# Three of five pairs of forms a step later: the order of VectorE in a fused attention and feed-forward kernel

## The chip, the core and the metric

The kernel runs on one core of a Trainium2 chip. Its metric is the device time in microseconds; the time before is the median of three runs. A profile is one further execution, recorded by the hardware profiler.

## What is computed

The first half is a recurrent attention (RWKV-6) with 4 batches, 8 heads, 768 tokens and heads of 48; the second half is a feed-forward layer on its result, all in float32.

```python
for t in range(S):                       # B=4, H=8, S=768, D=48
    cur = np.einsum('bhd,bhe->bhde', u[None] * kt, vt)
    y[:, :, t] = np.einsum('bhd,bhde->bhe', rt, state + cur)
    state = wt[:, :, :, None] * state + np.einsum('bhd,bhe->bhde', kt, vt)
...
x = y.transpose(0, 2, 1, 3).reshape(B * S, H * D)   # 3072 x 384
h = x @ w_in                                         # d_ff = 2048
g = h - np.tanh(h)
return (g @ w_out)
```

## The kernel before

**Blocks and steps.** The 3072 rows are cut into 8 blocks of 384 tokens (`blocks`, index `i`: four batches, two halves `q` each). The feed-forward of a block goes through 16 slices of 128 hidden columns (`f`, 0 to 15). One pass of the inner loop is a *step*: block `i`, slice `f`, numbered `now = 16 i + f`. While block `i` is in its feed-forward, the attention of block `i + 1` (`later`) is spread over the same 16 steps, and for `i + 2` (`after`) loads and scans begin. `plan(i)` says in which step which piece is issued: `phases` (TensorE and ScalarE work of the attention), `before` and `ahead` (the `prepare` calls, mostly long VectorE instructions), `loads`.

**The order is written by hand.** Under `tc.manual_schedule` each engine executes its instructions in the order in which the Python code issues them, so the place of a call in a step is its place in the queue of its engine. Waits between the engines follow from the data.

**One step.** TensorE does `hp = x @ w_in` for the slice (`first`, L749, three products that the profile counts as six instructions); `hp` has one PSUM buffer. ScalarE copies it to `h` (L752). `slight` then makes `g = h - tanh(h)` by a short polynomial that holds for small h: `s = h*h`, `qa = (s + c)^2`, `h = TOP*h*s`, `g = REST*qa*h`. The last two are VectorE instructions (L755). They are not issued in their own step but in the next one: `rest` keeps them. From block 2 on (`fast`), and for the first 10 slices of block 7, the square is ScalarE's (L770, with L771 and L773, a pass that checks the size of s). In blocks 0 and 1 and in the last six steps of block 7 the square is VectorE's (`square`, L778), issued in its own step; `qa` follows on ScalarE a step later.

**Second product.** In blocks 0, 1 and the end of block 7 it is plain (`Second`, L826): two steps after its slice TensorE adds `g @ w_out`. From block 2 on two neighbouring slices are taken together (`Fewer`): from the parts 0a 1a 2a of the even slice's `g` and 0b 1b 2b of the odd slice's (three token groups of 128) VectorE makes ten sums and differences, the *forms*, two in one instruction of 128 x 256 (`form_g`, L796, pairs 0, 2, 4, 6, 8):

```python
G_FORMS = (("sub", "1a", "0a"), ("sub", "1a", "2a"), ("add", 0, "1b"), ("add", 1, "1b"), ("sub", 2, "0b"),
           ("sub", 3, "2b"), ("sub", "2b", 4), ("sub", 5, "0b"), ("add", "2a", 3), ("add", 0, 6))
```

A number there is an earlier form. So pair 2 reads pair 0, pair 4 reads pair 2, pair 6 pair 4, pair 8 pair 6. Similar forms of `w_out` lie in `forms`. Fifteen products of 128 x 128 (`PRODUCTS`) replace eighteen. Twelve of them go into three PSUM banks (`acc`, four products to a bank, n // 4), in two halves (`add(q, part)`): in the kernel before first n = 0 to 5, which read forms 4 to 9, two steps after the odd slice, and then n = 6 to 11, which read forms 0 to 3 and the parts 0a and 2a, a step later. With the last pair of slices of a block `scaled` has ScalarE copy the banks out (L875). The other three (`others`) are issued together, at f = 9 and at the start of the next block. Then `SUMS` adds the products up (`sum`, L897) during steps 4 to 14 of the next block, and `store` writes them out.

**Buffers.** In the tile `G` (`g_at`) the forms 0 to 3 have two sets of slots by turns, the a parts two, the b parts four, the forms 4 to 9 one (slots 14 to 19). The accumulators have one buffer, the attention's PSUM scratch (`att`) two.

**VectorE's order in a step** is:

```python
for op in rest + behind + square + formed + extra:
    op()
```

`rest` is h and g of the slice before. `behind` holds VectorE's part of the attention work that TensorE did in the step before: the masked copies (`own`, `earlier`, L454), `update_2` (ten or eleven dependent instructions on the states, L533 and L543; issued at f = 11), `others_summed` (L890, f = 2). `formed` are the form pairs: pair 0 after an even slice, pairs 2, 4, 6 and 8 after an odd one. The `prepare` calls and `sum` come at the end of the step. The results of the attention (`result 1`, L586) are TensorE's work at f = 12; they write to the PSUM tiles that `update_2` reads.

Of the kernel before, what the change touches and what calls it, by code (L numbers as in the profile page):

```python
# [46 lines left out]
ALU = mybir.AluOpType  # L47
# [3 lines left out]
B, H, S, D = 4, 8, 768, 48  # L51
P = 128
# [44 lines left out]
G_FORMS = (("sub", "1a", "0a"), ("sub", "1a", "2a"), ("add", 0, "1b"), ("add", 1, "1b"), ("sub", 2, "0b"),  # L97
           ("sub", 3, "2b"), ("sub", "2b", 4), ("sub", 5, "0b"), ("add", "2a", 3), ("add", 0, 6))
# [5 lines left out]
AHEAD_N, MAIN = 6, 12  # L104
# [16 lines left out]
def kernel(  # L121
# [12 lines left out]
    nc = tc.nc  # L134
# [65 lines left out]
    states = []  # L200
# [80 lines left out]
    class Block:  # L281
# [241 lines left out]
                                                 rhs=self.v[toks, c, e0:e0 + D], start=True, stop=True)  # L523

        def update_2(self):
            St = states[self.q]

            def tot(c):
                by = self.whole().rearrange("d (p c) -> d p c", c=NCH)[:, :, c]
                return by.unsqueeze(2).to_broadcast([P, NPAIR, D])  # L530

            def product(out, in0, c):
                nc.vector.tensor_tensor(out=out, in0=in0, in1=tot(c), op=ALU.mult)  # L533

            if self.q > 0:
                product(St[:, :, 0, 0:D], St[:, :, 0, 0:D], 0)
            for c in range(NCH - 1 if self.q == NQ - 1 else NCH):
                dst = St[:, :, c + 1, 0:D] if c + 1 < NCH else states[self.q + 1][:, :, 0, 0:D]
                kv = self.kv[c].rearrange("d (p e) -> d p e", e=D)
                if self.q == 0 and c == 0:  # L540
                    product(dst, kv, 1)
                    continue
                nc.vector.tensor_tensor(out=dst, in0=St[:, :, c, 0:D], in1=kv, op=ALU.add)  # L543
                if c + 1 < NCH:
                    product(dst, dst, c + 1)

        def update_any(self, ps, p0, tot):
            ks, last = self.ks[:, p0:p0 + UP], self.q == NQ - 1
# [97 lines left out]
        def phase(self, ps, name):  # L646

            if name in ("own", "earlier"):
                return [getattr(self, name)(ps, p0) for p0 in HALVES]
            if name == "turn":  # L650
                for p0 in HALVES:
                    self.turn(ps, p0)
            elif name.startswith(("split", "turned", "join")):
                what, p0, *part = name.split()
                getattr(self, what)(int(p0), *(slice(int(x[0]), int(x[-1]) + 1) if what == "split" else
                                               range(int(x[0]), int(x[-1]) + 1) for x in part))
            elif name == "update":
                self.update_1(ps)
                return [self.update_2]
            elif name == "result 1":  # L660
                self.results(ps)
                self.result("from_states", ALL)
            elif name == "result 2":
                self.result("from_scores", ALL, True)
                self.result_out(ALL)
                self.fill_holes([nc.sync])
            return []
# [124 lines left out]
    def form_g(q, n):  # L792

        op, (a0, b0), (a1, b1) = G_FORMS[n][0], G_FORMS[n][1:], G_FORMS[n + 1][1:]
        to = g_at(q, n)
        return lambda: nc.vector.tensor_tensor(out=G[:, to:to + 2], in0=two(G, g_at(q, a0), g_at(q, a1)),  # L796
                                               in1=two(G, g_at(q, b0), g_at(q, b1)), op=OPS[op])
# [52 lines left out]
    class Fewer:  # L850
# [14 lines left out]

        def add(self, q, part):
            end = q == self.pairs - 1
            for n in (range(AHEAD_N), range(AHEAD_N, MAIN))[part]:
                self.product(self.acc[n // 4][:, n % 4 * P:(n % 4 + 1) * P], q, n, q == 0 and n % 4 == 0, end)
            if end:  # L870
                for bank in ((0,), (1, 2))[part]:
                    self.scaled(places(4 * bank, 4), self.acc[bank])

        def scaled(self, to, src):
# [16 lines left out]
                                           scalar=1.0 / UPSCALE, in1=self.half, op0=ALU.mult, op1=ALU.add)  # L891

        def sum(self, n, m):
            for op, *each in SUMS[n:m]:
                at = [two(sums, each[0][k], each[-1][k]) if len(each) == 2
                      else sums[:, each[0][k]:each[0][k] + 1] for k in range(3)]
                nc.vector.tensor_tensor(out=at[0], in0=at[1], in1=at[2], op=OPS[op])  # L897

        def pieces(self):
            for i, (a, b, c) in enumerate(PLACES):  # L900
# [62 lines left out]
    def boot(ps, blk, later):  # L963
# [41 lines left out]
        own()  # L1005
        blk.results(ps)
        blk.result("from_scores", both[0])
        blk.update_2()
        run(second_a)
        blk.result("from_states", ALL, cs=(0, 1), more=True)  # L1010
        earlier = blk.earlier(ps, h2)
# [29 lines left out]
    acc = [ps_d.tile([P, BANK], F32, name=f"acc{j}", tag=f"acc{j}") for j in range(NB // P)]  # L1041
    count = const.tile([P, 1], F32, name="count", tag="count")
    ahead_of_h, rest, formed, extra, behind, due, summed = [], [], [], [], [], [], []

    def sum_held(held, squares, over, to):

# [11 lines left out]
    for i, blk in enumerate(blocks):  # L1058
# [15 lines left out]
        for f in range(NF):  # L1074
# [4 lines left out]
                busy(acc[0], 2)  # L1079
            h, made = first(here, f, ps_d)  # L1080
            g, ahead_of_h, square, later_ops = slight(h, now, i, f)
            for op in rest + behind + square + formed + extra:
                op()
            rest, behind, formed = later_ops, [], []
            if not now:
                for op in fourth[0]:
                    op()
# [6 lines left out]
                extra = []  # L1094
            if f < few[i]:
                q = f // 2
                formed = [form_g(q, n) for n in (range(2, len(G_FORMS), 2) if f % 2 else (0,))]
                if f % 2:
                    due += [(now + 2, fewer.add, (q, 0)), (now + 2 + (f + 1 < few[i] or second is None), fewer.add, (q, 1))]
            else:  # L1100
                due.append((now + LAG + (not later), second.add, (f, g)))
            if fewer and f == 9:
                fewer.others(ps_a, range(4))
            if fewer and second:
                if f == 2 * LAST + 1:
                    fewer.others(ps_a, range(4, LAST))
                    behind.append(fewer.others_summed)
                elif f in (2 * LAST + 2, 2 * LAST + 3):
                    fewer.sum(*((0, 6) if f % 2 == 0 else (6, len(SUMS))))
# [6 lines left out]
            if later:  # L1116
                for name in before.get(f, ()):
                    later.prepare(name)
                for name in phases.get(f, ()):
                    behind += later.phase(ps_a, name)  # L1120
            if after:
                for name in ahead.get(f, ()):
                    after.prepare(name)
# [5 lines left out]
            some = ({4: (0, 2), 6: (2, 4), 8: (4, 6), 9: (6, 8), 14: (8, len(SUMS))} if later else  # L1129
                    {4: (0, 4), 6: (4, 8), 8: (8, len(SUMS))}).get(f)  # L1130
            if some and summed:
                summed[0].sum(*some)
                if some[1] == len(SUMS):
                    summed.pop().store()
# [107 lines left out]
```

## Time and profile before

| | |
|---|---|
| three timed runs | 567.73, 569.06, 571.91 us (median 569.06) |
| the profiled execution's own time | 567.05 us |
| its span, first to last instruction | 565.2 us |
| granted TensorE clock, mean | 0.999 |
| TensorE matmuls (PE) busy | 546.4 us, 97% |
| VectorE (DVE) busy | 477.3 us, 84% |
| ScalarE (ACT) busy | 376.8 us, 67% |
| hp products, L749 | 768 instructions, 488 ns each |
| products of the forms, L864 | 1350 instructions, 275 to 277 ns each |
| form pairs, L796 | 225 instructions, 424 ns each |
| h and g, L755 | 256 instructions, 549 to 558 ns each |
| blocks 2 to 7 begin | at 168.50, 231.38, 296.26, 361.17, 426.86, 492.48 us |

The profile's timeline gives for every instruction, or run of like ones, the start, the time that it took, the engine, the line of the program, the operation, what is written and read, the shape, and in brackets a longer idle time before it with what ended it. TensorE's instructions overlap, so that 275 ns each does not mean that they start 275 ns apart. PEld is TensorE's loading of weights, SPq a DMA issue.

### The profile page before, as it was taken

Reading aid. Unit: us, or ns where it says so; the run is one execution under the profiler, and the core shown is the slowest. Engines: PE = TensorE matmul, PEld = TensorE weight load, DVE = VectorE, ACT = ScalarE, POOL = GpSimd, SP = SyncE. Lnnn points to the kernel's source line nnn. Section 1 sums busy time; section 2 is a strip of 40 time slices with the busy share of each in tenths; the row PEclk is TensorE's granted clock in tenths of the full one; section 3 lists DMA queues with packets and bytes.
Section 4 is the critical chain, followed back from the end, with each engine's and each line's share of the span. In section 5 each row is a group of like instructions: output and inputs, shape, how many; then the busy total and the mean of one; then the engine's idle time right before and its main releaser. Section 6 shows DMA issues by size and latency. Waiting matters only on the chain.

```text
span 565.2 us, 13965 instructions
## 1 busy us (share of the span) xinstructions
PE 546.4 (97%) x5664; PEld 398.3 (70%) x5664; DVE 477.3 (84%) x926; ACT 376.8 (67%) x743; POOL 11.8 (2%) x40
## 2 busy tenths in 40 slices
PE   4889999999999999999999999999999999999996
PEld 4646666565665787877777777877877787787863
DVE  8888884799879989989999999989899998758673
ACT  3979893355337886588766886677865886566450
POOL 6100000000000000000000000000000000000000
PEclk9999999999999999999999999999999999999999
DMA  8596553244202532035302531126122320100101
GB/s 305 198 337 210 182 174 119 84 112 106 92 12 97 131 111 67 4 97 143 112 22 76 140 114 60 52 86 156 57 68 81 83 64 1 55 1 1 44 0 45
DMA packets 51268, 55.10 MB, mean 97 GB/s; under 512 B 21376, under 2 KB 49152, under 8 KB 51200
## 3 DMA queue, kind: packets, MB, share of 16 engines
q1 hardware_dynamic: 50960, 54.10, 31.6%
q8 instruction: 45, 0.74, 0.5%
q14 instruction: 23, 0.19, 0.1%
q0 software_dynamic: 96, 0.07, 0.1%
q10 hardware_dynamic: 144, 0.00, 0.0%
HBM read 43.55 MB, written 4.72 MB: 85 GB/s over the span
## 4 chain that ended last, share of the span: by engine, by line
PE 87%; DVE 6%; ACT 3%; DMA 2%; issue 1%; SPq 0%; DVEq 0%
PE hp L749 40%; PE acc L864 20%; PE acc L826 13%; PE att L864 5%; PE att L447 3%; PE att L586 2%; PE att L603 2%; PE att L521 2%; DVE g L796 1%; ACT up L255 1%; DMA r<-in_rT 1%; DMA w<-in_wT 1%; PE att L471 1%; DVE g L755 1%; DVE post L401 1%
## 5 line engine op out<-in xcount | busy, mean ns | idle before, releaser
L749 PE MATMUL hp<-xT,w_sb 128*128 128x384 f32 x768 | 270.1, 488 | 2.0 <-ACT h L752 1.4
L749 PEld LDWEIGHTS hp<-xT,w_sb 128*128 128x128 f32 x768 | 138.4, 190 | 81.8 <-ACT h L752 4.5
L752 ACT ACTIVATE h<-hp 128x384 f32<-128x384 f32 x128 | 62.8, 490 | 116.4 <-PE hp L749 114.7
L864 PE MATMUL acc<-forms,g 128*128 128x128 f32 x810 | 121.0, 277 | 0.5
L864 PEld LDWEIGHTS acc<-forms,g 128*128 128x128 f32 x810 | 109.1, 192 | 16.9 <-issue 1.2
L796 DVE TENSOR_TENSOR g<-g 128x256 f32<-128x256 f32 x225 | 95.4, 424 | 19.1 <-PE acc L864 0.5
L755 DVE SCALAR_TENSOR_TENSOR h<-h,s 128x384 f32<-128x384 f32 x128 | 70.3, 549 | 7.2 <-ACT s L770 6.6
L826 PE MATMUL acc<-w_sb,sums 128*128 128x384 f32 x192 | 68.1, 491 | 1.4 <-DVE sums L755 1.1
L755 DVE SCALAR_TENSOR_TENSOR g<-qa,h 128x384 f32<-128x384 f32 x96 | 53.6, 558 | 16.2 <-PE acc L864 2.7
L771 ACT ACTIVATE qa<-s,shift 128x384 f32<-128x384 f32 x90 | 55.4, 616 | 3.0
L773 ACT ACTIVATE junk<-s,shift 128x384 bf16<-128x384 f32 x90 | 54.0, 599 | 0.0
L826 PEld LDWEIGHTS acc<-w_sb,sums 128*128 128x128 f32 x192 | 35.7, 190 | 25.8 <-DVE sums L755 2.2
L770 ACT ACTIVATE s<-h 128x384 f32<-128x384 f32 x90 | 47.1, 523 | 2.8
L864 PE MATMUL acc<-w_sb,g 128*128 128x128 f32 x270 | 44.9, 275 | 0.0
L864 PEld LDWEIGHTS acc<-w_sb,g 128*128 128x128 f32 x270 | 37.4, 192 | 0.0
L781 ACT ACTIVATE qa<-s,shift 128x384 f32<-128x384 f32 x38 | 23.4, 617 | 19.3 <-DVE top L778 19.3
L255 ACT ACTIVATE up<-raw 128x768 f16<-128x768 f32 (+1 forms) x32 | 32.0, 1070 | 0.0
L755 DVE SCALAR_TENSOR_TENSOR sums<-qa,h 128x384 f32<-128x384 f32 x32 | 17.9, 558 | 15.6 <-ACT qa L781 12.4
L778 DVE CUSTOM_DVE_ANT_0 s<-h 128x384 f32<-128x384 f32 x38 | 21.0, 553 | 11.7 <-ACT h L752 11.7
L864 PE MATMUL att<-w_sb,g 128*128 128x128 f32 x180 | 30.2, 275 | 0.0
L864 PEld LDWEIGHTS att<-w_sb,g 128*128 128x128 f32 x180 | 26.4, 192 | 4.5
L387 DVE TENSOR_TENSOR_SCAN post<-w,seed 128x780 f32<-128x780 f32 x16 | 28.5, 1783 | 0.7 <-DMA w<-in_wT 0.6
(90 smaller groups left out, 549.3 us busy)
## 6 DMA issues: line engine op xcount, KB each, us to landing
raw<-in_weights SPq DMA_DIRECT2D x16, 768.0 KB, 4.4
w<-in_wT SPq DMA_DIRECT2D x7, 780.0 KB, 4.5
k<-in_kT SPq DMA_DIRECT2D x7, 768.0 KB, 4.4
r<-in_rT SPq DMA_DIRECT2D x7, 768.0 KB, 4.4
v_sb<-in_v SPq DMA_DIRECT2D x8, 576.0 KB, 4.3
k<-in_tokens SPq DMA_DIRECT2D x6, 576.0 KB, 3.9
r<-in_tokens SPq DMA_DIRECT2D x6, 576.0 KB, 4.8
out_y<-sums SPq DMA_DIRECT2D x15, 128.0 KB, 1.9
```

The costliest lines, as they stand in the source:

```text
L255: return lambda: nc.scalar.activation(out=to, in_=of, func=AF.Copy, scale=scale, bias=bias)
L387: return nc.vector.tensor_tensor_scan(out=back(t[:, 0:width]), data0=back(self.tile("w")[:, a:a + width]), data1=back(seed[:, 0:width]), i ...
L749: nc.tensor.matmul(hp, lhsT=w_in_sb[:, f, kc, :], rhs=xT[kc], start=(kc == KC - 1), stop=(kc == 0))
L752: return h, nc.scalar.activation(out=h, in_=hp, func=AF.Copy, scale=1.0 / UPSCALE)
L755: return lambda: nc.vector.scalar_tensor_tensor(out=out, in0=in0, scalar=scalar, in1=in1, op0=op0, op1=ALU.mult)
L770: nc.scalar.activation(out=s, in_=h, func=AF.Square)
L771: nc.scalar.activation(out=qa, in_=s, func=AF.Square, bias=shift[:, 4:5])
L773: nc.scalar.activation(out=junk[:, 0:NB], in_=s, func=AF.Relu, bias=shift[:, 5:6], accum_out=excess[:, at:at + 1])
L781: first = [lambda: nc.scalar.activation(out=qa, in_=s, func=AF.Square, bias=shift[:, 4:5])]
L796: return lambda: nc.vector.tensor_tensor(out=G[:, to:to + 2], in0=two(G, g_at(q, a0), g_at(q, a1)), in1=two(G, g_at(q, b0), g_at(q, b1)), ...
L826: nc.tensor.matmul(acc, lhsT=g[:, j * P:(j + 1) * P], rhs=w_out_sb[:, f, :], start=(f == self.first), stop=(f == NF - 1))
L864: nc.tensor.matmul(to, lhsT=G[:, g_at(q, a), :], rhs=rhs, start=start, stop=stop, skip_group_check=True)
```

## The change

In blocks 2 to 7, pairs 4, 6 and 8 of the forms are issued a step later than before and alternate with h and g: 4, h, 6, g, 8, then pair 0 of the next pair of slices. Pair 2 stays where it was. Since forms 4 to 9 now come later, the halves of the twelve products change places: first n = 6 to 11 (with bank 2 complete after it), then n = 0 to 5 (banks 0 and 1). The `prepare` calls, except `bound` (ScalarE), and the `sum` pieces move from the end of the step into the list at its start, and so does the splitting of `update_2` into single instructions; in steps without pairs 4, 6 and 8 these alternate with h, g and the form pair. In steps with a VectorE square, in block 1 and at the end of block 7, the square comes between h and g of the slice before. Block 0 keeps its order. The instructions are the same in number and size.

```diff
         def update_2(self):
-            St = states[self.q]
+            St, ops = states[self.q], []
...
-            def product(out, in0, c):
-                nc.vector.tensor_tensor(out=out, in0=in0, in1=tot(c), op=ALU.mult)
+            def step(out, in0, in1, op):
+                ops.append(lambda: nc.vector.tensor_tensor(out=out, in0=in0, in1=in1, op=op))
...
+            return ops
...
             elif name == "update":
                 self.update_1(ps)
-                return [self.update_2]
+                return self.update_2()
...
-            for n in (range(AHEAD_N), range(AHEAD_N, MAIN))[part]:
-                self.product(self.acc[n // 4][:, n % 4 * P:(n % 4 + 1) * P], q, n, q == 0 and n % 4 == 0, end)
+            for n in (range(AHEAD_N, MAIN), range(AHEAD_N))[part]:
+                self.product(self.acc[n // 4][:, n % 4 * P:(n % 4 + 1) * P], q, n, q == 0 and n in (0, AHEAD_N, 8),
+                             end)
             if end:
-                for bank in ((0,), (1, 2))[part]:
+                for bank in ((2,), (0, 1))[part]:
                     self.scaled(places(4 * bank, 4), self.acc[bank])
...
+    held_back, forming = [], []
+
+    def between(ops, others):
+
+        n = min(len(ops), len(others))
+        return [op for pair in zip(ops, others) for op in pair] + ops[n:] + others[n:]
...
-            for op in rest + behind + square + formed + extra:
+            some = ({4: (0, 2), 6: (2, 4), 8: (4, 6), 9: (6, 8), 14: (8, len(SUMS))} if later else
+                    {4: (0, 4), 6: (4, 8), 8: (8, len(SUMS))}).get(f) if summed else None
+            spare = summed[0].sum(*some) if some else []
+            if i:
+                for of, names in ((later, before.get(f, ())), (after, ahead.get(f, ()))):
+                    spare += [lambda of=of, name=name: of.prepare(name) for name in names
+                              if of and not name.startswith("bound")]
+            if not i:
+                ops = rest + behind + square + formed + extra
+            elif forming:
+                ops = between(forming, rest) + square + formed + behind + spare
+            elif square:
+                ops = rest[:1] + square + rest[1:] + formed + behind + extra + spare
+            else:
+                ops = between(rest + formed, behind + spare)
+            for op in ops:
                 op()
-            rest, behind, formed = later_ops, [], []
+            rest, behind, formed, forming, held_back = later_ops, [], [], held_back, []
...
             if f < few[i]:
                 q = f // 2
-                formed = [form_g(q, n) for n in (range(2, len(G_FORMS), 2) if f % 2 else (0,))]
+                formed = [form_g(q, 2 * (f % 2))]
                 if f % 2:
+                    held_back = [form_g(q, n) for n in range(4, len(G_FORMS), 2)]
                     due += [(now + 2, fewer.add, (q, 0)), (now + 2 + (f + 1 < few[i] or second is None), fewer.add, (q, 1))]
```

More of the change, by code (lines that the diff above doesn't have):

```diff
@@ L530, in tot @@
                 return by.unsqueeze(2).to_broadcast([P, NPAIR, D])
-            def product(out, in0, c):
-                nc.vector.tensor_tensor(out=out, in0=in0, in1=tot(c), op=ALU.mult)
+            def step(out, in0, in1, op):
+                ops.append(lambda: nc.vector.tensor_tensor(out=out, in0=in0, in1=in1, op=op))
             if self.q > 0:
-                product(St[:, :, 0, 0:D], St[:, :, 0, 0:D], 0)
+                step(St[:, :, 0, 0:D], St[:, :, 0, 0:D], tot(0), ALU.mult)
             for c in range(NCH - 1 if self.q == NQ - 1 else NCH):
@@ L540, in update_2 @@
                 if self.q == 0 and c == 0:
-                    product(dst, kv, 1)
+                    step(dst, kv, tot(1), ALU.mult)
                     continue
-                nc.vector.tensor_tensor(out=dst, in0=St[:, :, c, 0:D], in1=kv, op=ALU.add)
+                step(dst, St[:, :, c, 0:D], kv, ALU.add)
                 if c + 1 < NCH:
-                    product(dst, dst, c + 1)
+                    step(dst, dst, tot(c + 1), ALU.mult)
+            return ops
         def update_any(self, ps, p0, tot):
@@ L893, in sum @@
         def sum(self, n, m):
+            ops = []
             for op, *each in SUMS[n:m]:
@@ L896, in sum @@
                       else sums[:, each[0][k]:each[0][k] + 1] for k in range(3)]
-                nc.vector.tensor_tensor(out=at[0], in0=at[1], in1=at[2], op=OPS[op])
+                ops.append(lambda op=op, at=at: nc.vector.tensor_tensor(out=at[0], in0=at[1], in1=at[2], op=OPS[op]))
+            return ops
         def pieces(self):
@@ L1007, in boot @@
         blk.result("from_scores", both[0])
-        blk.update_2()
+        run(blk.update_2())
         run(second_a)
@@ L1108 @@
                 elif f in (2 * LAST + 2, 2 * LAST + 3):
-                    fewer.sum(*((0, 6) if f % 2 == 0 else (6, len(SUMS))))
+                    for op in fewer.sum(*((0, 6) if f % 2 == 0 else (6, len(SUMS)))):
+                        op()
                 elif f == 2 * LAST + 4:
@@ L1115 @@
                 sum_held(holds[:, at:at + n_top - 2], top[:, 0:n_top - 2], holds[:, 0:at + n_top - 2], ends[:, 0:1])
[L1116 to L1123, printed above, removed]
+            for of, names in ((later, before.get(f, ())), (after, ahead.get(f, ()))):
+                for name in names if of else ():
+                    if not i or name.startswith("bound"):
+                        of.prepare(name)
+                if of is later:
+                    for name in phases.get(f, ()) if later else ():
+                        behind += later.phase(ps_a, name)
             if fast and i == 1 and f >= 4 and f - 4 < len(W_FORMS):
@@ L1128 @@
                 form_w(n, 4)
[L1129 to L1134, printed above, removed]
+            if some and some[1] == len(SUMS):
+                summed.pop().store()
             name, ins = loads.get(f), None
```

## The prediction, made before the result was known

> **Names.** A step is one (block, f), b5 f12 say; T is the start of its first hp matmul. "Form pair 0, 2, 4, 6, 8" is the VectorE addition made by form_g with that number. Rows are start, duration, engine, line, operation.
>
> **What bounds the kernel now.** I read the page first, then TensorE's own timeline step by step, then VectorE's, then what each late piece waits for. The page's first two parts:
>
> ```profile
> PE 546.4 (97%) x5664; PEld 398.3 (70%) x5664; DVE 477.3 (84%) x926; ACT 376.8 (67%) x743; POOL 11.8 (2%) x40
> ...
> PE   4889999999999999999999999999999999999996
> ...
> DVE  8888884799879989989999999989899998758673
> PEclk9999999999999999999999999999999999999999
> ```
>
> TensorE is full from the fourth slice on, at full clock; VectorE is nearly full too. The timelines of TensorE and ScalarE around b3 f2 and f3:
>
> ```profile
> 240.61 2.10 PE L749 MATMUL hp<-xT,w_sb 128*128 128x384 f32 x6
> ...
> 243.89 2.10 PE L749 MATMUL hp<-xT,w_sb 128*128 128x384 f32 x6
> ...
> 244.95 1.06 ACT L875 ACTIVATE sums<-acc 128x512 f32<-128x512 f32 x2
> ...
> 245.83 1.05 PE L864 MATMUL acc<-forms,g 128*128 128x128 f32 x8
> ...
> 247.16 2.10 PE L749 MATMUL hp<-xT,w_sb 128*128 128x384 f32 x6
> ```
>
> A step without attention work lasts 3.275 us (247.16 - 243.89), hp first, then six products from T + 1.94. All such steps of blocks 2 to 7 last this long, those of block 7 too, where VectorE has half its work; so it is TensorE's floor. Against steps of the same kind only these are longer: b5 f4 by 0.30 (5.326 against 5.031), b6 f4 by 0.21, b5 f12 by 0.52 (7.310 against 6.789), b6 f12 by 0.54. Together 1.57 us: **all that a better order of VectorE can win**. Both places wait for VectorE. Here is f12, which waits for the last addition of update_2 (the results use the PSUM tile that it reads):
>
> ```profile
> 411.72 0.35 DVE L543 TENSOR_TENSOR states<-states,att 128x192 f32<-128x192 f32 x1
> ...
> 412.22 1.61 PE L586 MATMUL att<-pre,states 48*64 48x64 f32 x92 [0.23 <-DVE states L543]
> ```
>
> The addition ends at 412.07, while hp of that step (T 409.62) was done at T + 1.94 = 411.56: late by 0.51, and the step is 0.52 longer. So the wait is (end of the last addition) - (T + 1.94), near enough.
>
> Why VectorE is late there: h of the last step begins 2.23 us after T in b3 f0 (233.61 - 231.38), 3.31 in b4 f0, 4.41 in b5 f0. It loses 1.1 us a block. Where:
>
> ```profile
> 372.82 0.56 DVE L755 SCALAR_TENSOR_TENSOR g<-qa,h 128x384 f32<-128x384 f32 x1
> 373.30 0.55 DVE L890 SCALAR_TENSOR_TENSOR sums<-att,o 128x384 f32<-128x384 f32 x1
> 373.77 2.00 DVE L796 TENSOR_TENSOR g<-g 128x256 f32<-128x256 f32 x4
> 375.69 0.55 DVE L755 SCALAR_TENSOR_TENSOR h<-h,s 128x384 f32<-128x384 f32 x1
> 376.37 0.56 DVE L755 SCALAR_TENSOR_TENSOR g<-qa,h 128x384 f32<-128x384 f32 x1
> 377.03 0.42 DVE L796 TENSOR_TENSOR g<-g 128x256 f32<-128x256 f32 x1
> 377.38 1.75 DVE L394 TENSOR_TENSOR pre<-r,pre 128x1536 f32<-128x1536 f32 x1
> ```
>
> Four form pairs of 0.42 take 2.00: each begins 0.10 after the end of the one that it reads, 0.53 from start to start. An instruction that does not read its predecessor begins 0.08 before its end: pair to L394 0.35, g to the sums 0.48, and the first form pair, which reads the g two places ahead, 0.47 after the sums. A result two places back costs nothing.
>
> The Trainium skill (VectorE: DVE Perf Modes, section "The DRAIN you can't avoid") says otherwise: the next operation does not start until the pipe is empty, with or without semaphores between. By it alternating saves nothing; here the rows disagree (0.35 against 0.53), so I go by them and keep the rule's case as a rival.
>
> **The change part by part.**
>
> *Alternation.* In steps with forming the order is 4, h, 6, g, 8, 0: 0.34 + 0.47 + 0.34 + 0.47 + 0.34 + 0.34 = 2.30. The same six took h 0.68, g 0.66, pair 0 0.35 and three chained pairs of 0.53, 0.53, 0.35: 3.10. That is 0.8 a pair of steps, 6.4 a block, over five times the 1.1 that VectorE loses. The lateness goes, and with it the waits at f4: **-0.51**, and the old ones at f12: **-1.06**. Bounds: 0 and -1.57, which no saving on VectorE can pass.
>
> *Pair 4 now leads its step.* It overwrites slots 14 and 15 of G, which are single. The halves have changed places, so they are read by the first two products of the last six of the step before; pair 4 waits for them and h, g and everything behind wait with it. In a plain step these are done at about T + 2.6, before h can start (h waits for ScalarE's s, T + 3.2): free. At f10 the 80 or 96 kv matmuls (1.6 us) stand ahead: the products begin at T + 3.57 (274.82 - 271.25) and the first four records end at T + 4.28. With 0.09 from release to start, step f11 runs from T(f10): pair 4 at 4.37, h 4.71, pair 6 5.18, g 5.52, pair 8 5.99, pair 0 6.33, first update 6.67. In b3 the update takes 3.86 from its first start to the last addition's end (276.57 to 280.43): 10.53. TensorE wants it at T(f12) + 1.94 = 5.02 + 3.275 + 1.94 = 10.23. A new wait of 0.31, now in each of b2 to b6: **+1.55**. (Before, b3 had 1.05 to spare.) Bounds per block: 0, if something frees pair 4 early, and 1.05, if each of the six starts 0.04 after its predecessor, as the update's links do, instead of 0.08 before.
>
> *Halves changed.* At f1 and f2 of b3 to b7 the last six-packs of the block before end, and ScalarE empties the banks: before, bank 0 after f1, banks 1 and 2 after f2; now bank 2, then 0 and 1. The next block's first products, at f3, begin before with bank 0 (long empty), now with bank 1, the second of the two copies. These sit behind ScalarE's passes over f2: 244.95 to 246.01. TensorE wants the bank at 245.83. With 0.05 to start, 0.23, and 0.10 for the weight load that no longer hides (b2 f3, begun after a wait, is 3.377 long): 0.33 a block, **+1.65**. Bounds: 0.18 and 0.45 each.
>
> *Block 1.* There `square` now stands ahead of g and of `behind`. At f11 `behind` is the update:
>
> ```profile
> 145.53 0.35 DVE L533 TENSOR_TENSOR states<-att,whole 128x192 f32<-128x192 f32 x1
> ...
> 147.64 0.49 ACT L752 ACTIVATE h<-hp 128x384 f32<-128x384 f32 x1 [2.62 <-PE hp L749]
> ...
> 149.11 0.35 DVE L543 TENSOR_TENSOR states<-states,att 128x192 f32<-128x192 f32 x1
> 149.38 0.55 DVE L778 CUSTOM_DVE_ANT_0 s<-h 128x384 f32<-128x384 f32 x1
> ```
>
> The update ran while ScalarE's h was still to come. Now the square waits for that h (148.13 + 0.04 = 148.17), g follows at 148.65, the update at 149.12, and 3.93 later, at 153.05, its last addition ends. TensorE wants it at 149.38 + 1.94 = 151.32: **+1.73**, bounds 1.5 and 1.9. g itself is due two steps on and stays in time at every step (nearest: b1 f5, ended 123.41, due 124.60, now some 0.6 later).
>
> *Tail.* In b7 f15 g(14) slips ahead of the sum that the last check's matmul waits for (end 553.29, used 553.63): the sum ends about 553.64 and the matmul about 0.12 later, **+0.12**, bounds 0 and 0.3.
>
> *At nothing.* The moved prepare calls and sums issue no DMA; `behind` issues one GpSimd memset of 0.1 on an engine 2% busy; stores and loads keep their place. times_before (f3) keeps the same work ahead of it: after h at T(f2) + 3.2 come four starts (1.62) and its own 1.75, and at T(f2) + 6.6 it is 1.9 ahead of its use (T(f4) + 1.94, two plain steps on). Pair 2 is due a step after it, pairs 4 to 8 too. In b7 f11, where both halves fall into one step, pair 8 would end near 537.1 and is read at 538.7. The cover everywhere is VectorE's regained time; were it gone, f4 and f12 would pay again what they pay now.
>
> Sum: -1.57 + 1.55 + 1.65 + 1.73 + 0.12 = **+3.5 us**: span 568.7, and the profiled execution's own 567.05 becomes 570.5. The three timed runs lie 0.7, 2.0 and 4.9 above that execution; the median of all four is 568.4, and I add the sum to that: **571.9**, +0.6%. A measurement of this kernel can tell about 1% from no change, so I call it no change, on the slow side.
>
> **Rivals.**
>
> *Every VectorE start waits for the end ahead* (slower). Place: f11 of b2 to b6, behind pair 4. With chained prices, 4.37 + 0.53 + 0.68 + 0.53 + 0.66 + 0.53 + 0.53 = 7.83, last addition at 11.69, wait 1.47 a block, 7.35 in all: +9.3, **577.7**. It decides once the six average over 0.50 from start to start. For it: h to g and pair to pair do cost this today. Against it: the 0.35 and 0.47 above. This is what the skill's section named above would give.
>
> *Only the gain and block 1.* Pair 4 and bank 1 are released in time: matmul ends are modelled in the profile, and ScalarE may reach its copies sooner. -1.57 + 1.73 + 0.12 = +0.3, **568.7**. Against it: g of b2 f11 started 0.09 after the modelled end that it waited for.
>
> *Gain alone.* Block 1's update is not held: -1.6 or a little under, **566.8**. Against it: the code puts `square` ahead of `behind` in every step of that block.
>
> *More than the idle is won* (faster by over 1%). It needs steps under 3.275, and nothing shown is.
>
> *It does not do what it says*: pairs 4 to 8 stay chained because an added wait ends late anyway. Then VectorE stays late; sum near the forecast's, since the new waits of TensorE give it the time: about 572.
>
> **How the numbers follow.** Forecast 0.58, chained 0.16, gain and block 1 0.13, gain alone 0.06, not as said 0.04, over 1% faster 0.03. Over 1% slower means +5.7: the chained case and the upper bounds of the forecast's update wait (5.3 instead of 1.55), together 0.21. Faster by over 1% 0.03; the rest, 0.76, within 1%. The range runs from the gain alone to just under the chained case: 567.0 to 577.0; the forecast's own is 569.5 to 575.
>
> **What would show it.** Right: f4 of b5 and b6 back at 5.03; f12 of b2 to b6 each 0.3 over 6.79; f3 of b3 to b7 near 3.6; b1 f12 near 9.1 instead of 7.41; VectorE's h no later after T in b5 f0 than in b3 f0. Wrong: update rows that begin earlier than T(f10) + 6, a bank-1 product that follows hp at once, or any plain step that is longer.

## The result, and the profile after

The changed kernel takes 572.97 us (median of 22 runs, 570.05 to 577.59), the kernel before 567.84 us (22 runs beside them, 566.48 to 571.91). The ratio is 1.008, with a 95% interval of 1.0056 to 1.0104: **slower by 4.5 us**, between 3.2 and 5.9. The forecast said 571.9 (569.5 to 575 as the forecast's own range), +0.6%, no change on the slow side. The time is close, closer than the change: the forecast added its 3.5 to a base of 568.4, and the kernel before measured 567.84 in the 22 runs, so a base that was 0.6 too high hid part of what the sum had missed. That part is luck. Of the 5.74 us that the profiles show (below), 3.3 are terms of the forecast; the rest is two things that the prediction had not seen.

The first parts of the page of the changed kernel, with its group of form pairs:

```profile
PE 552.5 (96%) x5664; PEld 399.8 (69%) x5664; DVE 453.5 (79%) x926; ACT 376.5 (65%) x743; POOL 11.9 (2%) x40
...
PEclk9689999999989999999999999999999999999998
...
L797 DVE TENSOR_TENSOR g<-g 128x256 f32<-128x256 f32 x225 | 90.7, 419 | 44.3 <-PE acc L865 42.6
```

VectorE was to be relieved, and it was: 453.5 us busy instead of 477.3, with the same 926 instructions. TensorE got nothing for it. Ahead of the form pairs VectorE now stands idle for 42.6 us waiting for TensorE's products (0.5 before): that is pair 4 at the head of its step. And PEclk, which has a 9 in every slice of the kernel before, has dents: a 6 and an 8 in the second and third slices, an 8 in the twelfth and one at the very end.

The profiled execution took 577.57 us with a span of 575.9, 10.6 more than the span of before. Almost half of that is not the change's: in this execution the clock was at one half from 19.9 to 33.5 us, so that the first hp product began at 33.39 us instead of 27.87. That part of the program was not touched, and runs of the kernel before with a low mean clock are longer as well (0.987 and 572.27 us, beside 0.998 and 567.5). So **I compare from the start of b0 f4 to the end**: 522.47 us before, 528.20 after, +5.74. Step by step (from the start of one step's first hp product to the next one's), all differences over 0.06 us from there on:

| step | before | after | difference | forecast |
|---|---|---|---|---|
| b1 f12 | 7.410 | 10.847 | +3.44 | +1.73 |
| b2 f7 | 3.275 | 4.053 | +0.78 | 0 |
| f12 of b2, b3, b4 | 6.788 to 6.789 | 7.036 to 7.076 | +0.25 to +0.29 | +0.31 |
| f12 of b5, b6 | 7.310, 7.329 | 7.039, 7.040 | -0.27, -0.29 | -0.21, -0.23 |
| f4 of b5, b6 | 5.326, 5.241 | 5.031, 5.030 | -0.30, -0.21 | -0.30, -0.21 |
| f3 of b3 to b7 | 3.275 | 3.613 to 3.614 | +0.34 each | +0.33 each |
| b7 f15 with the tail | 15.561 | 15.712 | +0.15 | +0.12 |

Block 1 first. TensorE's timeline of the changed kernel from the step ahead of b1 f12 on:

```profile
154.26 2.10 PE L750 MATMUL hp<-xT,w_sb 128*128 128x384 f32 x6
156.45 0.33 PE L587 MATMUL att<-pre,states 48*64 48x64 f32 x4
158.08 1.61 PE L587 MATMUL att<-pre,states 48*64 48x64 f32 x92 [1.30 <-DVE states L533]
159.80 3.89 PE L827 MATMUL acc<-w_sb,sums 128*128 128x384 f32 x6
```

VectorE's timeline of the changed kernel in the same stretch:

```profile
148.99 0.55 DVE L756 SCALAR_TENSOR_TENSOR h<-h,s 128x384 f32<-128x384 f32 x1
153.05 0.56 DVE L779 CUSTOM_DVE_ANT_0 s<-h 128x384 f32<-128x384 f32 x1 [3.50 <-ACT h L753]
...
153.53 0.55 DVE L756 SCALAR_TENSOR_TENSOR sums<-qa,h 128x384 f32<-128x384 f32 x1
154.00 0.35 DVE L533 TENSOR_TENSOR states<-att,whole 128x192 f32<-128x192 f32 x1
...
157.58 0.35 DVE L533 TENSOR_TENSOR states<-states,att 128x192 f32<-128x192 f32 x1
```

The square stands idle for 3.50 us until ScalarE's h comes, and g and the ten instructions of the update wait behind it, though nothing that they need is missing. The update then ends at 157.93, and the results on TensorE, which had begun with four products, wait 1.30 us for it. That is the forecast's mechanism at the forecast's place and price: the end is 3.67 us after T (154.26), and so is the forecast's (153.05 after 149.38). Then comes what was not forecast: six products of `Second` take 3.89 us in that row. Busy time and granted clock in three stretches of 3.41 us:

```profile
core 0: us, PE busy (x) PEld busy (x) DVE busy (x) ACT busy (x) POOL busy (x), PEclk, DMA share, GB/s
156.42:159.84 3.42, 1.99 (x97) 1.77 (x97) 3.21 (x7) 0.47 (x1) 0.00 (x0) 1.00 0.18 61
159.84:163.25 3.41, 3.41 (x6) 1.80 (x6) 3.41 (x6) 0.00 (x0) 0.00 (x0) 0.50 0.00 0
163.25:166.66 3.41, 3.41 (x103) 2.43 (x102) 1.53 (x4) 1.75 (x5) 0.00 (x0) 1.00 0.02 5
```

For 3.41 us, right behind the wait and the 92 thin products that follow it, TensorE's granted clock is 0.50. The wait cost 1.7 and the half clock another 1.7 (experiment 2 has the first without the second).

The second surprise is b2 f7. VectorE's timeline of the changed kernel there:

```profile
200.31 0.54 DVE L756 SCALAR_TENSOR_TENSOR h<-h,s 128x384 f32<-128x384 f32 x1
202.47 1.36 DVE L347 TENSOR_TENSOR k<-k,r 128x1152 f32<-128x1152 f32 x1 [1.62 <-DMA r<-in_tokens]
203.75 0.55 DVE L756 SCALAR_TENSOR_TENSOR g<-qa,h 128x384 f32<-128x384 f32 x1
204.33 0.42 DVE L797 TENSOR_TENSOR g<-g 128x256 f32<-128x256 f32 x1
```

L347 is one of the moved `prepare` calls (`product_r`), and it reads a tile that a DMA fills. It now stands ahead of g and pair 2, and holds both for 1.62 us until the load has landed. TensorE needs the pair, in its own timeline of the changed kernel:

```profile
202.20 2.10 PE L750 MATMUL hp<-xT,w_sb 128*128 128x384 f32 x6
204.81 0.71 PE L865 MATMUL acc<-forms,g 128*128 128x128 f32 x4 [0.51 <-DVE g L797]
```

The load is no later than before: SyncE issued it at 197.35, 4.85 us ahead of T, and at 189.02 in the kernel before, 4.86 ahead of T (193.88). But there VectorE came to L347 only after the four chained pairs, at T + 0.73, and did not wait. VectorE's timeline of the kernel before:

```profile
192.68 2.01 DVE L796 TENSOR_TENSOR g<-g 128x256 f32<-128x256 f32 x4
194.61 1.35 DVE L347 TENSOR_TENSOR k<-k,r 128x1152 f32<-128x1152 f32 x1
```

In the changed kernel VectorE reaches it ahead of the load, and g and pair 2 now stand behind it.

The wait for the bank, in b3 f3, again on TensorE:

```profile
253.28 2.10 PE L750 MATMUL hp<-xT,w_sb 128*128 128x384 f32 x6
255.45 0.71 PE L865 MATMUL acc<-forms,g 128*128 128x128 f32 x4
...
256.89 0.49 PE L750 MATMUL hp<-xT,w_sb 128*128 128x384 f32 x1
```

and on ScalarE, whose two copies of the banks (L877) are shown here as one run:

```profile
254.33 1.06 ACT L877 ACTIVATE sums<-acc 128x512 f32<-128x512 f32 x2
```

The second copy ends at 255.39 and the product begins at 255.45, 2.17 after T instead of 1.94.

And VectorE around the update at f11 of b3 in the changed kernel (T of f10 is 280.97, T of f12 289.27):

```profile
285.30 0.43 DVE L797 TENSOR_TENSOR g<-g 128x256 f32<-128x256 f32 x1 [3.57 <-PE acc L865]
285.64 0.55 DVE L756 SCALAR_TENSOR_TENSOR h<-h,s 128x384 f32<-128x384 f32 x1
286.11 0.42 DVE L797 TENSOR_TENSOR g<-g 128x256 f32<-128x256 f32 x1
286.44 0.55 DVE L756 SCALAR_TENSOR_TENSOR g<-qa,h 128x384 f32<-128x384 f32 x1
286.91 0.75 DVE L797 TENSOR_TENSOR g<-g 128x256 f32<-128x256 f32 x2
287.58 0.35 DVE L533 TENSOR_TENSOR states<-att,whole 128x192 f32<-128x192 f32 x1
...
291.09 0.35 DVE L533 TENSOR_TENSOR states<-states,att 128x192 f32<-128x192 f32 x1
```

Pair 4 starts at T(f10) + 4.33 (forecast 4.37), the update at + 6.61 (6.67), and its last addition ends at 291.44, + 10.47 (10.53). The first five instructions of the alternation start 0.34, 0.47, 0.33 and 0.47 after one another: the price forecast, not the 0.53 of the chain.

### The profile page after: what moved, and what is told of

Read it like the earlier page. It is cut to its first block, busy times and chain, and to the rows that moved or that the text cites. A ratio compares the mean times of both kernels' runs of the same rounds, so it can differ in the third digit from the quotient of the medians.

```text
span 575.9 us, 13925 instructions
## 1 busy us (share of the span) xinstructions
PE 552.5 (96%) x5664; PEld 399.8 (69%) x5664; DVE 453.5 (79%) x926; ACT 376.5 (65%) x743; POOL 11.9 (2%) x40
## 4 chain that ended last, share of the span: by engine, by line
PE 87%; DVE 4%; ACT 4%; issue 2%; DMA 2%; SPq 0%; ACTq 0%; DVEq 0%
PE hp L750 39%; PE acc L865 20%; PE acc L827 13%; PE att L865 5%; PE att L587 3%; PE att L447 2%; PE att L604 2%; PE att L521 2%; DVE states L533 1%; DMA r<-in_rT 1%; DMA r<-in_tokens 1%; ACT h L753 1%; ACT sums L877 1%; ACT junk L774 1%; DVE post L387 1%
## 5 line engine op out<-in xcount | busy, mean ns | idle before, releaser
L797 DVE TENSOR_TENSOR g<-g 128x256 f32<-128x256 f32 x225 | 90.7, 419 | 44.3 <-PE acc L865 42.6
L827 PE MATMUL acc<-w_sb,sums 128*128 128x384 f32 x192 | 69.7, 500 | 0.7 <-DVE sums L756 0.5
L376 DVE TENSOR_TENSOR_SCAN pre<-w,start 128x780 f32<-128x780 f32 x16 | 28.5, 1783 | 0.6
```

Of the source, the lines that this page charges most:

```text
L376: return nc.vector.tensor_tensor_scan(out=self.tile("pre")[:, cols], data0=self.tile("w")[:, cols], data1=start[:, 0:n * NCH * LP], initia ...
L827: nc.tensor.matmul(acc, lhsT=g[:, j * P:(j + 1) * P], rhs=w_out_sb[:, f, :], start=(f == self.first), stop=(f == NF - 1))
```

## The experiments

The theory after the result: four places, each with an instruction at the head of VectorE's or ScalarE's queue that waits for something while urgent work stands behind it, account for all of the loss: the square ahead of b1's update (with the clock as its consequence), bank 1 emptied second, pair 4 ahead of the update, and `product_r` ahead of g. The rivals: the alternation itself costs, the exchange of the halves costs, or the four are not independent and something else is late next. Times are again from the start of b0 f4 to the end, in one profiled execution each (528.20 for the changed kernel, 522.47 for the kernel before), unless runs are named.

**1. The square back behind the update.**

```diff
             elif square:
-                ops = rest[:1] + square + rest[1:] + formed + behind + extra + spare
+                ops = rest + behind + square + formed + extra + spare
```

> Block 1 (and the end of block 7) gets back the order in which h, g and the update stand ahead of the square; all else as in the changed kernel. Theory: the update no longer waits for ScalarE's h, so step b1 f12 falls from 10.85 us to 7.41, by 1.63 of waiting and 1.7 of the half clock that followed the wait, and no half clock is granted near it; the other long steps stay (f3 3.61, f12 of b2 to b6 7.04, b2 f7 4.05). Time about 3.4 below the changed kernel in the same state. Rival 1, the clock drops there by itself: b1 f12 falls only to about 9.1 (7.41 + 1.7). Rival 2, VectorE is too late in block 1 anyhow: no change.

Measured: 524.64. b1 f12 is 7.410 us, as before the change, and its clock stays whole. The other three remain: b2 f7 3.97, f3 3.61, f12 7.04. Timed in 10 runs it takes 569.92 us against 567.60 (13 runs), ratio 1.0039 (1.0021 to 1.0057). The square's place was worth 3.44 us here, and the half clock goes with the wait.

**2. Bank 1 copied out first.**

```diff
-                for bank in ((2,), (0, 1))[part]:
+                for bank in ((2,), (1, 0))[part]:
```

> At a block's end ScalarE empties bank 1 ahead of bank 0; all else as in the changed kernel. Theory: bank 1 is then empty 1.6 us after the start of f3 instead of 2.1, and the products want it at 1.94: f3 of b3 to b7 falls from 3.61 to 3.275, 1.7 us in all, and bank 0, wanted a step later, costs nothing. Rival, the products of f3 wait for something of VectorE: f3 stays at 3.61. b1 f12 keeps its wait; whether the half clock follows it again shows if it belongs to the wait (10.8) or fell there by chance (9.1).

Measured: 524.52. All five f3 are 3.275 again: which of two banks is copied first was worth 0.34 us a block. f7 of b2, which the edit does not touch, is 3.72 instead of 4.05; I come back to that. But b1 f12 came out at 9.16, although this edit does not reach block 1. TensorE's timeline of this kernel there:

```profile
151.86 0.33 PE L587 MATMUL att<-pre,states 48*64 48x64 f32 x4
153.49 1.62 PE L587 MATMUL att<-pre,states 48*64 48x64 f32 x92 [1.30 <-DVE states L533]
155.21 2.20 PE L827 MATMUL acc<-w_sb,sums 128*128 128x384 f32 x6
```

The same wait, to the hundredth, and then 2.20 us for the six products instead of 3.89. So the wait and the half clock are two things, and the second does not always follow the first.

**3. The update ahead of the held pairs.**

```diff
             elif forming:
-                ops = between(forming, rest) + square + formed + behind + spare
+                ops = (rest + behind + forming if f == 11 and later else between(forming, rest) + square)
+                ops += formed + (spare if f == 11 and later else behind + spare)
```

> At f11 of blocks 2 to 6 the order is h, g, update, then pairs 4, 6, 8 and pair 0; all else as in the changed kernel. Theory: the update no longer stands behind pair 4, which waits for TensorE's products of f10; its last addition ends near T(f10) + 8.3 instead of 10.5, and f12 of b2 to b6 falls from 7.04 to 6.79 (b2: 7.08), 1.3 us in all. Rival 1, the order inside f11 is not what delays the update (VectorE is late as a whole): f12 stays. Rival 2, the pairs, now later, hold up TensorE's second half at f12: f12 becomes longer than 7.04.

Measured: 526.78. f12 of b2 to b6 is 6.786 to 6.789, the floor that b2 to b4 had before the change, and b5 and b6 now have it as well. b1 f12 is 10.78, with the half clock again; b2 f7 is 3.80.

**4. The `prepare` calls and sums back to the end of a step.**

```diff
             else:
-                ops = between(rest + formed, behind + spare)
+                ops = between(rest + formed, behind) + spare
```

> In steps without pairs 4, 6 and 8 the prepare calls and sums stand behind h, g and the form pair instead of between them (the masked copies and the sum of the other products still alternate); all else as in the changed kernel. Theory: in b2 f6 the product with r, which waits for a DMA, no longer stands ahead of g and pair 2, so step b2 f7 falls from 4.05 to 3.275, 0.8 us; nothing else gets longer, since VectorE has time now. Rival 1, pair 2 is late for another reason: f7 of b2 stays at 4.05. Rival 2, the lost overlap makes VectorE late: f4 or f12 of b4 to b6 get longer by 0.2 or more.

Measured: 526.20. b2 f7 is back at 3.275; b1 f12 9.17 without the half clock; f3 and f12 as in the changed kernel, but for f12 of b3 (7.404) and b4 (7.127), 0.36 and 0.09 longer. In b4 the update ends 2.27 us after T instead of 2.18, and the results begin later by as much. In b3 the update ends where it does elsewhere; there the 96 attention products of L604 take 1.92 us instead of 1.56, and the profile names no wait for them. What that is stays open.

**5. All four together.**

> All four edits together: block 1's order as before, bank 1 emptied first, the update ahead of the pairs at f11, prepare calls and sums last. What stays of the change is pairs 4, 6, 8 a step later and alternating, and the halves exchanged. Theory: every new wait is gone and the old ones too, so no step is longer than its kind (plain 3.275, f4 5.03, f12 6.79, b1 f12 7.41, b2 f7 3.275), and from b0 f4 to the end the profile shows 520.9 us (522.47 - 1.57), against 528.2 of the changed kernel and 522.5 before: ratio to before 0.997. Rival 1, alternation costs something not seen yet: 522.5 or more, ratio 1.000 or above. Rival 2, more than the idle is won: plain steps under 3.275.

Measured: 520.86, and **every step is at the length of its kind**: b1 f12 7.408, b2 f7 3.275, f3 3.275, f4 5.030, f12 6.788. Against the changed kernel that is -7.34; the single edits give -3.44 - 0.78 - 5 x 0.34 - 5 x 0.25 = -7.17, and the tail (15.571 instead of 15.712) most of the rest. Timed in 12 runs it takes 565.97 us against 567.73 (17 runs), ratio 0.9971 (0.995 to 0.9992): **this version beats both kernels**, the one before by 1.6 us in the profile (522.47 - 520.86) and 1.76 by the medians. VectorE's timeline at f11 of b3 in it:

```profile
275.83 0.56 DVE L756 SCALAR_TENSOR_TENSOR h<-h,s 128x384 f32<-128x384 f32 x1 [1.59 <-ACT s L771]
276.52 0.56 DVE L756 SCALAR_TENSOR_TENSOR g<-qa,h 128x384 f32<-128x384 f32 x1
277.00 0.35 DVE L533 TENSOR_TENSOR states<-att,whole 128x192 f32<-128x192 f32 x1
...
280.57 0.35 DVE L533 TENSOR_TENSOR states<-states,att 128x192 f32<-128x192 f32 x1
280.85 1.81 DVE L797 TENSOR_TENSOR g<-g 128x256 f32<-128x256 f32 x4
```

and what TensorE does with it:

```profile
280.90 2.10 PE L750 MATMUL hp<-xT,w_sb 128*128 128x384 f32 x6
282.93 1.63 PE L587 MATMUL att<-pre,states 48*64 48x64 f32 x96
```

h, g and the update no longer stand behind pair 4's wait for TensorE. The update ends at 280.92, two microseconds ahead of its use, and the results follow hp without a gap.

**6. The changed kernel, with its held pairs chained instead of alternating.**

```diff
-                ops = between(forming, rest) + square + formed + behind + spare
+                ops = rest + forming + square + formed + behind + spare
```

> Pairs 4, 6 and 8 still come a step later, but behind h and g and one after the other, not alternating; all else as in the changed kernel. Theory: pairs take 0.53 from start to start again (0.34 alternating), but h and g no longer stand behind pair 4 and its wait, so the update begins 0.5 earlier after f10 (6.1 instead of 6.7): f12 of b2 to b6 back to 6.79 to 6.85, and VectorE still keeps up, since 2.9 us for six instructions is 0.2 under the order of before, with 0.2 more won at pair 2; f4 5.03. Rival (each start waits for the end ahead anyway, so alternating won nothing): pairs take the same start to start as in the changed kernel, f12 unchanged at 7.04. Rival 2, VectorE falls behind without alternation: f4 and f12 of b5 and b6 longer than 5.2 and 7.2.

Measured: 525.03. f12 is 6.79, f4 5.03, b1 f12 9.16 without the half clock, f3 3.61. VectorE is busy for 464.1 us instead of 453.5, and its h begins 2.40 us after T in b5 f0. With h and g ahead of the pairs, the update does not suffer even with the pairs chained (0.53 from start to start): what costs at f12 is not the chain's price but pair 4 as the first of the step. The update ends 1.69 us after T instead of 2.18, though it still stands behind the pairs.

**7. The kernel before, with nothing but the square moved in block 1.**

```diff
-            for op in rest + behind + square + formed + extra:
+            for op in (rest[:1] + square + rest[1:] + behind + formed + extra if i == 1 else
+                       rest + behind + square + formed + extra):
```

> The kernel before with one part of the change alone: in block 1 the square stands between h and g, ahead of the update. Theory: this part by itself makes b1 f12 9.15 us (no half clock) or 10.8 (half clock after it) instead of 7.41; blocks 2 to 7 as before, f12 of b5 and b6 7.3. Rival, the wait needs VectorE's other new order: b1 f12 stays at 7.41.

Measured: 526.89. b1 f12 is 10.71 with the half clock, so that the move can do all of it by itself, without anything else of the change. TensorE's timeline of this kernel:

```profile
153.53 1.77 PE L586 MATMUL att<-pre,states 48*64 48x64 f32 x92 [1.30 <-DVE states L543]
155.40 3.59 PE L826 MATMUL acc<-w_sb,sums 128*128 128x384 f32 x6
```

Not expected: the old waits of b5 and b6, which this edit does not touch, changed by +0.42 and +0.02 (f12) and +0.01 and +0.39 (f4), and b4 f15 by +0.10. The waits hang on how late VectorE happens to be.

**8. The halves of the products back in their old places.**

```diff
-            for n in (range(AHEAD_N, MAIN), range(AHEAD_N))[part]:
-                self.product(self.acc[n // 4][:, n % 4 * P:(n % 4 + 1) * P], q, n, q == 0 and n in (0, AHEAD_N, 8),
+            for n in (range(AHEAD_N), range(AHEAD_N, MAIN))[part]:
+                self.product(self.acc[n // 4][:, n % 4 * P:(n % 4 + 1) * P], q, n, q == 0 and n % 4 == 0,
...
-                for bank in ((2,), (0, 1))[part]:
+                for bank in ((0,), (1, 2))[part]:
```

> The changed kernel with the halves of the products in their old places (n = 0 to 5 first, banks 0, then 1 and 2), so that forms 4 to 9 are read in the step in which VectorE makes them. Theory: f3 of b3 to b7 falls to 3.275, as bank 0 comes first again; pair 4 is read by products of a step before and no longer holds h, g and the update back, so f12 of b2 to b6 falls to 6.79; plain steps stay at 3.275 where VectorE is not late (pair 8 ends near T + 1.7 and is read from T + 2.8). Late steps (f13, f15 behind update and scans) may wait up to 0.5 each. Rival: the halves had to change places, TensorE now waits for pairs 4 to 8 at every odd step, plain odd steps 3.6 or longer, more than 10 us in all. b1 f12 9.15 or 10.8 as before in both.

Measured: 527.69. f3 and f12 are at their floors (3.275, 6.79), but now f7 of b2 to b6 is 5.56, 3.84, 3.89, 3.78 and 4.20. The first products of a step then read pairs 4 to 8 in the very step in which VectorE makes them, and behind `product_r` they come too late. Neither the theory, which had late steps at f13 and f15, nor the rival, which had every odd step late, named f7. From the list of waits of this kernel:

```profile
DVE k L347 <- DMA r<-in_tokens: 4.2, 5, 2.1
```

Five waits for that load, 4.2 us in all, instead of one of 1.62.

**9. The same, with the square and the `prepare` calls back as in 1 and 4.**

> Halves of the products in their old places, block 1's order as before, prepare calls and sums last: no update edit and no bank edit is needed then. Theory: the product with r still waits for its DMA until about 0.1 into f7 and takes 1.27, so pairs 4, 6 and 8 begin 1.4 into f7 and are read from 1.94, 2.39 and 2.83 on: f7 of b2 to b6 longer by 0.5 to 0.9 each, some 3 us in all, all other steps of their kind (f3 3.275, f12 6.79, b1 f12 7.41); from b0 f4 to the end 523 to 525 us. That is what the exchange of the halves is for. Rival, f7 is late only because the product with r stood ahead of g: f7 back at 3.275 and 520.9 in all.

Measured: 525.37. b1 f12 is 7.41, yet f7 of b2 to b6 is still 4.51, 3.85, 3.95, 3.85 and 4.06, and b4 f15 3.69. `product_r` begins between 0.06 us ahead of T and 0.16 behind it in these f7 and takes 1.36, so that pair 4 begins only at T + 1.22 or later; in b4 f15 the sums stand ahead of it, and it begins at T + 1.06. The last products of the step then wait for pair 8. So the old halves go with pairs that come a step later only where no long instruction of VectorE stands ahead of those pairs. **With VectorE's other work where it is, the exchange of the halves is needed** (the same f7 is 3.275 in 5); its price of 0.34 a block came only from the order of two copies. Whether the old halves would do with `product_r` in another step was not run.

**10. The wait of b1 f12 covered on TensorE.** The changed kernel, with the six products of `Second` that are due in that step issued ahead of the results instead of behind them:

```diff
+            while now == NF + 12 and due and due[0][0] <= now:
+                _, add, what = due.pop(0)
+                add(*what)
```

> The changed kernel, but in b1 f12 TensorE adds the product of slice 10 ahead of the attention's results instead of behind them; VectorE's order is that of the changed kernel. Theory: the 1.94 us of the product cover the 1.63 us of waiting for the update, so b1 f12 is 7.41 to 7.5, and with TensorE never idle there no half clock follows; the rest as in the changed kernel (f3 3.61, f12 7.04, b2 f7 3.7 to 4.1). Rival, VectorE's own lateness in block 1 is what costs: later steps of block 1 or f3, f4 of block 2 get longer, or b1 f12 stays over 8.5.

Measured: 525.13, b1 f12 7.92. TensorE's timeline:

```profile
149.48 2.10 PE L750 MATMUL hp<-xT,w_sb 128*128 128x384 f32 x6
151.41 2.10 PE L827 MATMUL acc<-w_sb,sums 128*128 128x384 f32 x6
153.44 1.63 PE L587 MATMUL att<-pre,states 48*64 48x64 f32 x96
155.21 0.99 PE L604 MATMUL att<-scores,v_sb 64*48 64x64 f32 x54
156.60 0.87 PE L604 MATMUL att<-scores,v_sb 64*48 64x64 f32 x42 [0.40 <-issue]
```

The late update costs nothing when 2.0 us of other work stand ahead of the results: no wait for the states, and no half clock. All of the 0.51 us that the step is still over 7.41 lies in the products of L604, which take 2.27 us from the first start to the last end instead of 1.56; 0.40 of that is the idle time in the last row, which the profile puts down to no wait. They are the same group of products as in b3 of 4.

**11. The edits without alternation.** As 5, but the pairs a step later are chained behind h and g as in 6, at f = 11 too, where the update then stands behind them.

> Block 1's order as before, bank 1 first, prepare calls and sums last, and pairs 4, 6, 8 a step later but one after the other behind h and g, without alternating. Theory: TensorE does not need the alternation; VectorE saves 0.2 at pair 2 and 0.2 at h and g in each two steps and wins the 1.1 us a block that it lost before: no step is longer than its kind, 520.9 us from b0 f4 to the end, as with all four edits. Rival, the saving is in the alternation alone: VectorE loses time from block to block again, h of the last step more than 3 us after the start of b5 f0, and f4 or f12 of b5 and b6 are 0.2 to 0.5 longer, 521.5 to 522.5.

Measured: 521.07 against 520.86 for 5; f12 6.79 but for b3 (6.87) and b4 (6.91), where the update is in time and the L604 products are longer again, f4 5.03, f3 3.275. VectorE is busy for 471.4 us instead of 462.1, and its h begins 3.27 us after T in b5 f0. So the old waits go when three of the five pairs come a step later; that they alternate relieves VectorE by some 9 us more, for which TensorE has no use.

## Why the prediction was right, and where it was wrong

**The gain, -1.57: right.** f4 of b5 and b6 are at 5.03, and h of b5 f0 begins 1.62 us after T instead of 4.41: the lateness is gone. The sign that the forecast named for this, no later in b5 f0 than in b3 f0, is not met to the letter (1.10 in b3, 1.22 in b4, 1.62 in b5, 1.22 in b6), but nothing adds up from block to block any more. That nothing more could be won was right too; 5, with every wait gone, wins 1.6 us.

**Alternation at 0.34 and 0.47 a start: right.** The rival in which every VectorE start waits for the end ahead (577.7) is refuted by the rows at f11 above. With it, for these instructions, goes the sentence that the prediction weighed from the Trainium skill (VectorE: DVE Perf Modes, "The DRAIN you can't avoid"), taken without exception; the section itself adds that a next operation that is not held starts earlier, and the prediction left that out. The total says it too: the same instructions are 453.5 us busy alternating and 464.1 chained (6).

**Pair 4 at the head of its step, +0.31 a block: right in the mechanism** (3 and 6 remove it) and nearly in size, 0.25 (0.29 in b2, where 0.03 of it lies in the L604 products).

**Bank 1, +0.33 a block: right**, 0.34. Experiment 2 shows that it is the order of the copies.

**Block 1, +1.73: right for the wait, too small for the step.** Where the wait came alone, the step is 9.16 to 9.17, against the 9.14 that the sum gives. In the profiled execution it was 10.85. The step that failed is the sum's silence on the clock: "span 568.7" was worked out with every matmul at full clock. 7 shows that the square's place alone can bring both, and 2, 4, 6 and 8 that the half clock does not always come.

**At nothing, the moved `prepare` calls: wrong, +0.78 in b2 f7.** This is the plain step that is longer, one of the forecast's own signs of being wrong. The prediction checked which DMAs these calls issue, and found none. It did not ask which DMA they wait for. It counted VectorE's regained time as the cover; here that time does harm, since VectorE reaches `product_r` 1.62 us ahead of its load. The place ahead of g is what makes it cost: in 4, with `product_r` last, VectorE still waits 0.38 us for the load, and the step is 3.275. The size changes with the execution: the six kernels with this order (the changed one, 1, 2, 3, 6 and 10) have 3.72 to 4.05 there. In 8, where pairs 4 to 8 are urgent too, the same instruction waits in five blocks.

**Tail, +0.12: right**, 0.15. The length of the last step alone does not show it: 7, which leaves the tail's order as before, has 15.73 (15.56 before), and 3, with the new order, 15.86. But the last check's matmul starts 3.96 us after T in all six profiles with the old order (before, 1, 5, 7, 9 and 11) and 4.11 in all seven with the new one, and VectorE's last instruction 10.19 and 10.34 after T. What varies from execution to execution comes behind that instruction.

The terms that were in the sum, measured, make 3.3 with the wait of block 1 at 1.75; b2 f7 adds 0.78 and the clock 1.7, together 5.8 for the 5.74 of the profiled execution. Without the half clock of block 1, 4.1 is left. What the timed 4.5 holds of the clock stays open. The eight runs of the changed kernel with a mean clock of 0.997 or more have a median of 570.86; 23 of the 31 runs of the kernel before beside experiments 1, 5 and 9 have such a clock and a median of 567.54, 3.3 less. The other fourteen runs of the changed kernel, 0.983 to 0.995, take 571.33 to 577.59, and a half clock at the start of the program, as in the profiled execution, lowers the mean as one in block 1 does.

## What to carry to other kernels

Before moving work on an engine that executes in order, ask of each moved instruction what it waits for, not only what it costs: a square that waits for another engine, a product that waits for a load or a pair that waits for its slot to be read costs nothing at the end of a step, and holds all that stands behind it at the head. Time saved on an engine that is off the critical path is worth no more than the waits that the bounding engine has for it (in 5, 1.6 us for 15 us less busy time of VectorE), and it moves that engine's instructions to where their inputs are not there yet. Where an engine must come late, put other work of the waiting engine ahead of the late result (10), and empty first the buffer that is wanted first (2).

## What the runs showed of the hardware that was not expected

**A wait of 1.30 us with thin products behind it can halve TensorE's clock for 3.41 us.** Seven profiles hold the late results of b1 f12: 1.30 us of waiting, then 92 products of 48 x 64 (1.6 us). The clock fell to 0.50 behind them in three (the changed kernel, 3 and 7) and not in four (2, 4, 6 and 8), and cost 1.6 to 1.7 us where it fell. The records of the clock change at multiples of 3.413 us from one another. Where it fell, the stretch of that length ahead of the fall began 1.7 to 2.2 us after T and so held the wait and the thin products with at most 0.2 us of hp (done at T + 1.94); where it did not, the stretch that holds the wait, counted from the clock's other records, began 0.5 to 1.6 after T, with 0.4 us of hp or more in its first part. TensorE's busy time does not tell the two kinds apart: it is 1.98 to 2.03 of 3.41 us in all seven. The Trainium skill (TensorE: Matmul & The Clock Gate, "HAM oscillation — how this bites in real kernels") gives as the rule that gaps of TensorE should not pass about 3.4 us. Here 1.30 was enough, with thin products beside it, and in these seven executions the fall went with where the stretch happened to begin. Why, and where the boundary lies between 1.6 and 1.7, is not shown.

**Thin products have idle time of their own.** The L604 products of f12 had idle times of up to 0.4 us in 4 and 10 that the profile puts down to no wait. Smaller ones, 0.03 to 0.14 us a step, lie there in the changed kernel (b2), 9 (b3, b5), 10 (b5) and 11 (b3, b4). In the other steps the same 96 products take 1.56 us, and nothing in these runs explains the difference.
